# Four row tiles on GpSimd, 16-bit sine angles and a rearranged filter front in a gated-mixer kernel

## Chip, cores and metric

One core of a Trainium2 chip. The metric is the device time of one launch in microseconds (us). Engines are named as in the profile: PE is TensorE, PEld its weight loads, DVE is VectorE, ACT is ScalarE, POOL is GpSimd, SP is SyncE. "Clock" is the mean granted clock of TensorE over a run, 1.0 being full speed.

## The reference, cut to what matters

```python
def _A_ref(q, k, v, shift_k, ssm_k, ssm_D):      # S = 2048, D = 640, all bf16
    k_shift = sum(k_pad[:, t:t + S, :] * shift_k[:, 3 - t] for t in range(4))
    kv = k_shift * v
    y = irfft(rfft(kv, padded to 2S) * rfft(ssm_k, padded to 2S))[:S]
    return q * (y + kv * ssm_D)                  # ssm_D: the "skip weights"

def _B_ref(x, w1, b1, w2, b2):                   # x is q; w1: S x 1536, w2: 1536 x S
    h = layernorm(x, axis=-1)                    # 2048 rows of 640: 16 "row tiles" of 128 rows
    return transpose(gelu(einsum("bsd,sf->bdf", h, w1) + b1) @ w2 + b2)

g = sigmoid((x * gate_w).sum(-1))
return g * A + (1 - g) * B
```

## The kernel before

Transforms are matmuls against sine tables (FTB), which ScalarE makes out of integer angles (pint). Each of the five filter blocks of 128 channels is turned by eight transposes on PE and evicted into wT. A list scheduler with estimated durations fixes the order of every engine's instructions when the kernel is built; on the chip each engine then runs its list in order. These parts are touched by the change or by the argument (cuts marked):

```python
def ts(eng, o, a, s1, s2, op0, op1=None, mode=1, ...):      # tensor_scalar, one or two operations
    n = n_of(o)
    d = dve_dur(n, mode) + extra if eng == "DVE" else n / 900.0 + 0.2     # what the scheduler believes
    ...

SPIN = (7, 3, 3, 2, 2)          # "spins": matmuls on zeros ahead of the transposes of each block
...
for p in PORD:                  # angles of one sine block, int32
    pv = pint[:, p, :, 1, :]
    t_ = tt("DVE", pv, V(acol, ...), V(brow, ...), ALU.mult, mode=1)
    ts("DVE", pint[:, p, :, 0, :], pv, 1024.0, None, ALU.add, mode=2)
    pprev = ts("DVE", pa, pa, 4095, None, ALU.bitwise_and, mode=2)
    sins[p] = act(FTB[...], pa, ACT.Sin, ...)
...
def transp(h, db):              # f32 PSUM; the skip weight is folded in by a one-row matmul
    for kt in range(2):
        for p in range(4):
            dfold = h == 0 and kt == 0 and p == 0
            if dfold:
                items.append((o, ident[0:1, :], Drow[0:1, 128 * db:128 * db + 128], True, False))
            items.append((o, V(ssm, ...), ident[:, :], not dfold, True))
    m_ = mms(vt, (spin(SPIN[db]) if h == 0 else []) + items, name="wtr")
    o_ = act(V(wT, ...), ..., ACT.Copy, vt=vt, name="wT")
...
def ln_scale(a, b):             # rstd of tiles a..b-1, on GpSimd
    ts("POOL", sd[:, a:b], mv[:, a:b, 1], 1e-5, None, ALU.add, prio=0)
    tt("POOL", rstd[:, a:b], sd[:, a:b], V(cst, 1, [[0, n]]), ALU.pow, prio=0)
    ...
def ln_apply(a, b):             # normalise tiles, on VectorE
    for t in range(a, b):
        xs = X[:, t // 4, t % 4, :]
        o_ = ts("DVE", xs, xs, mv[:, t, 0:1], rstd[:, t:t + 1], ALU.subtract, ALU.mult, mode=4, ...)
...
for t in range(12):             # statistics of 12 tiles (two lines in the kernel)
    ln_tile(t // 4, t % 4)
ln_scale(0, 8); ln_apply(0, 8)
for t in range(12, 16):
    ln_tile(t // 4, t % 4)
ln_scale(8, 16); ln_apply(8, 16)
for g0 in KFP:                  # filter taps: four two-input products of 1120 elements
    tt("POOL", KF[:, g0:g0 + 5, :, :], V(cw, ...), V(m32, ...), ALU.mult, ...)
```

Of the kernel before, what the change touches and what calls it, by code (L numbers as in the profile page):

```python
# [10 lines left out]
F32 = mybir.dt.float32  # L11
I32 = mybir.dt.int32
ACT = mybir.ActivationFunctionType
ALU = mybir.AluOpType
# [4 lines left out]
class _Tracker:  # L19
# [31 lines left out]
    def regions(self, ap):  # L51
# [5 lines left out]
        apl = [tuple(p) for p in ap.ap]  # L57
        esz_ap = mybir.dt.size(ap.dtype)
        assert esz_ap == esize, "bitcast size change unsupported in tracker"
        off = ap.offset  # L60
# [8 lines left out]
        free = apl[1:]  # L69
# [213 lines left out]
    def mm(self, ps_ap, lhsT, rhs, start, stop, final_val, inc, transpose=False):  # L283
        acc_r = []
        for a in (lhsT, rhs):
            for r in self.regions(a):
                acc_r.append((r, "R"))
        acc = list(acc_r)
        ps_regs = self.regions(ps_ap)
        if start:  # L290
            for r in ps_regs:
                acc.append((r, "W"))
        need = self.deps_for("PE", acc)
        self.do_waits("PE", need)
        ins = self.nc.tensor.matmul(ps_ap, lhsT=lhsT, rhs=rhs, start=start, stop=stop, skip_group_check=True)  # L295
        src = ("eng", "PE", final_val)
        for reg, mode in acc_r:
            self.add_record(reg, "R", src)
        for r in ps_regs:
            self.add_record(r, "W", src)  # L300
        if inc:
            ins.then_inc(self.clk["PE"], 1)
            self.cnt["PE"] += 1
            assert self.cnt["PE"] == final_val, (self.cnt["PE"], final_val)
            self.hist["PE"].append(dict(self.known["PE"]))
        return ins
# [19 lines left out]
class _Sched:  # L326
# [59 lines left out]
    def run(self):  # L386
# [12 lines left out]
        pend = {e: [] for e in engs}  # L399
        free = {e: 2.4 if e == "ACT" else 0.0 for e in engs}  # L400
        port = {"DVE": 0.0, "POOL": 0.0}
        dma_free = 0.0
        avail = {}
# [108 lines left out]
def _build(nc, A_q, A_k, A_v, A_shift_k, A_ssm_k, A_ssm_D, B_x, B_w1, B_b1, B_w2, B_b2, gate_w, out):  # L512
# [10 lines left out]
    with ExitStack() as es:  # L523
# [60 lines left out]
        E_base = cur[0]  # L584
        acol = alloc("acol", [128, 2, 4], I32, at=base_of(SS))
        brow = alloc("brow", [128, 2, 128], I32, at=base_of(SS) + 64)
        dif = alloc("dif", [128, 128], I32, at=base_of(SS) + 64 + 1024)
# [7 lines left out]
        kv1 = alloc("kv1", [128, 2, 4, D], BF16, at=E_base)  # L595
        ksh = [alloc(f"ksh{i}", [128, 4, D], BF16, at=base_of(GT) + 5120 * (1 + i)) for i in range(2)]
        rows = alloc("rows", [20, 5, 512], BF16, at=base_of(GT))
        kn = [alloc(f"kn{i}", [128, 4, D], BF16, at=base_of(ring[1]) + 5120 * i) for i in range(2)]
        kp = [alloc("kp0", [128, NG, 128], BF16, at=base_of(ring[1]) + 10240), alloc("kp1", [128, NG, 128], BF16, at=base_of(GTB))]
        pint = alloc("pint", [128, 4, 2, 2, 256], I32, at=base_of(ring[1]))  # L600
        W2 = alloc("W2", [128, 32, 512], BF16, at=base_of(ring[0]))
# [77 lines left out]
        def last_stt(o, i, sc, b, vt):  # L679
# [3 lines left out]
            return SC.add("DVE", dve_dur(n_of(o), 1), emit, [sc, b], [o], vt=vt, name="fin")  # L683

        def memset(eng, ap, val, prio=None):
            return SC.add(eng, 0.2, lambda s: T.op(eng, lambda e: e.memset(ap, val), [], [ap]), [], [ap], prio=prio)  # L686

# [38 lines left out]
        def chk(ci):  # L726
            return lambda s: s[:, ci * 512:ci * 512 + 320]

        def ssm_load(h, a, b):
            dma(ssm[:, a:b, 1024 * h:1024 * h + 1024], dr(A_ssm_k, 128 * S * a + 1024 * h, [[S, 128], [128 * S, b - a], [1, 1024]]), 128 * (b - a) * 2048, chain=True, rate=(262.0 if a == 0 else 195.0) if h == 0 else 385.0)  # L730

# [6 lines left out]
        def x_load(hk):  # L738
            dma(X[:, hk, :, :], dr(A_q, 512 * hk * D, [[4 * D, 128], [1, 4 * D]]), 128 * 5120, chain=True, rate=410.0)

# [43 lines left out]
        memset("DVE", zz[:, :], 0.0, prio=-1)  # L784
        SPIN = (7, 3, 3, 2, 2)

        def spin(k):
            return [((lambda s: s[:, 0:512]), zz[:, 0:128], zz[:, :], True, True)] * k

        T_PI = float(np.float32(math.pi * (1.0 - 1e-6)))  # L790
        memset("DVE", cst[:, 0:1], T_PI)
        memset("DVE", cst[:, 1:2], -0.5)
        iota = lambda ap, pat, b, cm: SC.add("POOL", 0.2, lambda s: T.op("POOL", lambda e: e.iota(ap, pat, base=b, channel_multiplier=cm), [], [ap]), [], [ap])
        iota(dif[:, :], [[1, 128]], 0, -1)
        iota(acol[:, :, :], [[4, 2], [1, 4]], 0, 8)
        iota(brow[:, :, :], [[-512, 2], [4, 128]], 1, 0)
        iota(dif2[:, :], [[1, 32]], 128, -1)
        ts("DVE", ident[:, :], dif[:, :], 0.0, None, ALU.is_equal)
        memset("POOL", rows[0:20, 3:5, :].rearrange("g a b -> g (a b)")[:, 0:896], 0.0)
        ro, ri = V(rows, 1536, [[128, 4], [160, 4], [1, 32]], pn=20), V(rows, 0, [[1, 4], [0, 4], [4, 32]], pn=20)  # L800
        SC.add("DVE", 0.6, lambda s: T.op("DVE", lambda e: e.tensor_copy(ro, ri), [ri], [ro]), [ri], [ro], prio=0, name="taps")
        PORD = (0, 2, 1, 3)
        sins = {}
        for p in PORD:
            pv = pint[:, p, :, 1, :]
            t_ = tt("DVE", pv, V(acol, p, [[4, 2], [0, 256]]), V(brow, 0, [[0, 2], [1, 256]]), ALU.mult, mode=1)
            ts("DVE", pint[:, p, :, 0, :], pv, 1024.0, None, ALU.add, mode=2)
            pa = pint[:, p, :, :, :].rearrange("q a b c -> q (a b c)")
            if p != 0:
                t_.after.add(pprev)  # L810
            pprev = ts("DVE", pa, pa, 4095, None, ALU.bitwise_and, mode=2)
            pv3 = pa
            sins[p] = act(FTB[:, p, :, :, :, :].rearrange("q a b c d -> q (a b c d)"), pa, ACT.Sin, bias=cst[:, 0:1],
                scale=-(2.0 * math.pi / 4096.0) * (1.0 - 1e-6), name="sin")

        for hk in range(2):
# [15 lines left out]
        def consts():  # L832
# [6 lines left out]
            act(cc[:, :], lambda s: s[:, 0:28], ACT.Copy, vt=vt, name="cc")  # L839

        def transp(h, db):
            vt = _VT("cv")
            items = []
            for kt in range(2):
                for p in range(4):
                    o = (lambda s, j=4 * kt + p: s[:, 128 * j:128 * j + 128])
                    dfold = h == 0 and kt == 0 and p == 0
                    if dfold:
                        items.append((o, ident[0:1, :], Drow[0:1, 128 * db:128 * db + 128], True, False))
                    items.append((o, V(ssm, db * S + 1024 * h + 4 * kt + p, [[8, 128]]), ident[:, :], not dfold, True))  # L850
            m_ = mms(vt, (spin(SPIN[db]) if h == 0 else []) + items, name="wtr")
            m_.dur = 0.5
            o_ = act(V(wT, 2 * h * SL + 128 * db, [[SL, 2], [D, 4], [1, 128]]), (lambda s: s[:, :].rearrange("q (a b c) -> q a b c", a=2, b=4)), ACT.Copy, vt=vt, name="wT")
            if h == 0:
                o_.after.add(sins[0 if db == 0 else 2])

# [83 lines left out]

        MIXP = 330
        LNA = 8
        lnlast = []
        kfirst = []
        KFP = (0, 5, 10, 15)
        srcW = lambda h: (lambda kt, p, ci: wT[:, 2 * h + kt, p, 320 * ci:320 * ci + 320])
        for h in range(2):
            for db in range(ND):
                transp(h, db)
            if h == 0:  # L950
                consts()
# [6 lines left out]
            if h == 0:  # L958
                for t in range(8):
                    ln_tile(t // 4, t % 4)  # L960
                for t in range(8, 12):
                    ln_tile(t // 4, t % 4)
                lnlast.append(SC.ops[-1])
                ln_scale(0, LNA)
                ln_apply(0, LNA)
                lnlast.append(SC.ops[-1])
                for t in range(12, 16):
                    for o_ in ln_tile(t // 4, t % 4):
                        o_.after.update(lnlast[-1:])
                ln_scale(LNA, 16)  # L970
                ln_apply(LNA, 16)
                lnlast.append(SC.ops[-1])
                for g0 in KFP:
                    tt("POOL", KF[:, g0:g0 + 20 // len(KFP), :, :], V(cw, 7 * g0, [[7, 20 // len(KFP)], [1, 7], [0, 32]]), V(m32, 0, [[0, 20 // len(KFP)], [0, 7], [1, 32]]), ALU.mult, xr=[pv3] if g0 == 0 else []).after.update(kfirst[:1])
                    kfirst.append(SC.ops[-1])
                for hk in range(2):
                    k_turn(hk)
                mixing(C[0], SS, 0, fine=True, prio=MIXP)
            else:
                mixing(C[1], C[0], 0, conj=True, prio=MIXP)  # L980
# [338 lines left out]
```

## Time and profile before

| | before |
|---|---|
| median of 4 runs (range) | 181.96 us (181.78 to 183.0) |
| span of the profiled run, clock | 179.7 us, 1.0 |
| PE / DVE busy | 96% / 95% |
| last row tile normalised | 33.0 us |
| first eviction of the filter transform | 13.79 us |

The span in the trace is about 2 us shorter than the time of the launch. The lines of this profile are shown in the prediction.

To compare two kernels that do the same matmuls in another order I use one figure more: **matmul work done by a time t**. It is the number of 320-column matmuls begun by t, in PE's timeline, times 0.1362 us (about their pitch in unbroken runs there: 80 in 11.03 us, less the tail of the last), plus the number of key-convolution matmuls times 0.0545. Transposes and matmuls on zeros are left out. A kernel that has done 2 us less than another at the same t stands 2 us behind. It is an estimate worked out from counts.

### The profile page before, as it was taken

How to read it: one execution, taken by the hardware profiler on the slowest of the kernel's cores; microseconds unless marked ns; L12 is line 12 of the kernel's file. 1: busy time of each engine (PE TensorE's matmuls, PEld its weight loads, DVE VectorE, ACT ScalarE, POOL GpSimd, SP SyncE). 2: the span in 40 equal slices, each digit the busy share in tenths (PEclk: the TensorE clock that was granted, in tenths of full speed). 3: DMA queues.
4: the chain of work that ended last, by engine and by line, in shares of the span. 5: the costliest groups of instructions: out<-in, count | busy, mean ns of one | idle time of the engine just before them, and what ended most of it. 6: DMA issues, size and time to landing. Idle time of an engine off the chain costs nothing.

```text
span 179.7 us, 3335 instructions
## 1 busy us (share of the span) xinstructions
PE 173.1 (96%) x1381; PEld 128.7 (72%) x1381; DVE 171.2 (95%) x203; ACT 116.9 (65%) x176; POOL 43.7 (24%) x42
## 2 busy tenths in 40 slices
PE   7969998899999999999999999999999999999993
PEld 2546785587778777776777778888888887777772
DVE  7999895999999999999999899999999999999984
ACT  5899998899898999617999932131231323753760
POOL 4089404190000054000240010402525000252000
PEclk9999999999999999999999999999999999999999
DMA  6999999999999999998299969797999999599463
GB/s 151 381 411 372 388 294 194 268 420 296 212 258 286 184 271 248 229 228 218 60 243 299 197 94 365 170 225 253 166 193 217 210 200 385 218 154 240 116 233 135
DMA packets 38542, 43.51 MB, mean 242 GB/s; under 512 B 15867, under 2 KB 31360, under 8 KB 38528
## 3 DMA queue, kind: packets, MB, share of 16 engines
q1 hardware_dynamic: 33296, 32.16, 58.2%
q0 software_dynamic: 5200, 11.14, 35.6%
q8 instruction: 11, 0.18, 0.4%
q14 instruction: 3, 0.02, 0.0%
q10 hardware_dynamic: 32, 0.01, 0.0%
HBM read 25.87 MB, written 2.62 MB: 159 GB/s over the span
## 4 chain that ended last, share of the span: by engine, by line
PE 88%; ACT 10%; DVE 0%; issue 0%
PE pp L295 88%; ACT wT L670 3%; ACT C L670 2%; ACT ksh L670 2%; ACT FTB L670 2%; ACT L670 1%; ACT GT L670 0%; DVE O L682 0%; DVE zz L686 0%; ACT cw L670 0%; DVE cst L686 0%
## 5 line engine op out<-in xcount | busy, mean ns | idle before, releaser
L295 PE MATMUL pp<-X,ring 128*128 128x320 bf16 x384 | 55.6, 299 | 0.0
L626 DVE TENSOR_TENSOR C<-C 128x2560 bf16<-128x2560 bf16 (+2 forms) x37 | 54.5, 1521 | 0.0
L295 PE MATMUL pp<-GT,W 128*128 128x320 bf16 x384 | 52.6, 299 | 0.0
L295 PEld LDWEIGHTS pp<-GT,W 128*128 128x128 bf16 x384 | 43.6, 114 | 8.6
L295 PEld LDWEIGHTS pp<-X,ring 128*128 128x128 bf16 x384 | 37.1, 98 | 14.9 <-DVE X L641 0.7
L670 ACT ACTIVATE C<-pp 128x640 bf16<-128x640 f32 x64 | 40.4, 723 | 4.9 <-PE pp L295 4.9
L670 ACT ACTIVATE O<-pp,c,omg 128x640 bf16<-128x640 f32 x15 | 13.3, 884 | 34.7 <-PE pp L295 34.7
L264 POOL DMA_DIRECT2D C<-C x8 | 10.9, 1610 | 41.7 <-DVE C L626 38.3
L295 PE MATMUL pp<-wT,FTB 128*128 128x320 bf16 x112 | 17.2, 299 | 2.5 <-ACT wT L670 1.4
L670 ACT ACTIVATE cgb<-pp,gg 128x640 bf16<-128x640 f32 x16 | 12.7, 794 | 5.7 <-PE pp L295 5.3
L295 PEld LDWEIGHTS pp<-wT,FTB 128*128 128x128 bf16 x112 | 10.5, 98 | 7.7 <-ACT wT L670 1.8
L670 ACT ACTIVATE GT<-pp,cc 128x640 bf16<-128x640 f32 x12 | 9.6, 799 | 9.0 <-PE pp L295 9.0
L626 DVE TENSOR_TENSOR tm<-C,C 128x2560 bf16<-128x2560 bf16 (+1 forms) x7 | 14.3, 2057 | 0.0
L922 DVE BATCH_NORM_STATS2 stats<-X 128x6 f32<-128x320 bf16 x32 | 13.5, 461 | 0.0
L295 PE MATMUL pp<-C,FTB 128*128 128x320 bf16 x96 | 13.4, 299 | 0.0
L264 POOL DMA_DIRECT2D C<-q_hi x6 | 5.9, 977 | 27.7 <-DVE C L626 13.2
L295 PEld LDWEIGHTS pp<-C,FTB 128*128 128x128 bf16 x96 | 9.3, 98 | 3.8 <-issue 0.3
L670 ACT ACTIVATE gq<-gq 128x640 bf16<-128x640 bf16 x16 | 11.8, 741 | 0.0
L626 DVE TENSOR_TENSOR SS<-C 128x2560 bf16<-128x2560 bf16 x8 | 11.7, 1487 | 0.1
L626 DVE TENSOR_TENSOR C<-tm 128x2560 bf16<-128x2560 bf16 (+1 forms) x9 | 10.6, 1192 | 0.1
L670 ACT ACTIVATE ksh<-pp 128x1024 bf16<-128x1024 f32 (+1 forms) x12 | 9.8, 894 | 0.6 <-PE pp L295 0.6
L670 ACT ACTIVATE wT<-pp 128x1024 bf16<-128x1024 f32 x10 | 9.7, 1041 | 0.6 <-PE pp L295 0.6
(73 smaller groups left out, 193.4 us busy)
## 6 DMA issues: line engine op xcount, KB each, us to landing
ring<-in_B_w_dram SPq DMA_DIRECT2D x12, 512.0 KB, 9.6
W<-in_B_w_dram SPq DMA_DIRECT2D x12, 512.0 KB, 6.5
C<-C POOLq DMA_DIRECT2D x8, 640.0 KB, 10.6
X<-in_A_q_dram SPq DMA_DIRECT2D x4, 640.0 KB, 8.4
kn<-in_A_k_dram SPq DMA_DIRECT2D x4, 640.0 KB, 9.3
out_dram<-O SPq DMA_DIRECT2D x7, 320.0 KB, 3.5
C<-SS POOLq DMA_DIRECT2D x3, 640.0 KB, 11.4
ssm<-in_A_ssm_k_dram SPq DMA_DIRECT2D x3, 512.0 KB, 6.8
```

Source lines behind the costliest of these rows:

```text
L264: ins = engobj.dma_start(out_ap, in_ap, accum_op=ALU.add, max_dma_last_dim=2560)
L295: ins = self.nc.tensor.matmul(ps_ap, lhsT=lhsT, rhs=rhs, start=start, stop=stop, skip_group_check=True)
L626: o_ = SC.add(eng, d, lambda s: T.op(eng, lambda e: e.tensor_tensor(o, a, b, op), rd, [o]), rd, [o], prio=prio, name="tt")
L670: return T.op("ACT", lambda e: e.activation(o, src, func, **kw), rr + [src], ww)
L922: ops.append(SC.add("DVE", 0.38, (lambda o, i: lambda s: T.op("DVE", lambda e: e.bn_stats(o, i), [i], [o]))(o, i), [i], [o]))
```

## The change

The intent: take work off VectorE and ScalarE in the first 33 us, where TensorE still waits. GpSimd, 24% busy, normalises four of the sixteen row tiles while VectorE finishes all statistics; angles come from a 16-bit table; the filter is transposed into bf16 PSUM without the one-row matmul, so the skip weights are added to row 0 of wT afterwards; one filter block is evicted by VectorE; ten of the twenty matmuls on zeros go.

```diff
-        SPIN = (7, 3, 3, 2, 2)
+        SPIN = (0, 3, 0, 0, 0)                   # and four spins ahead: SP0 = 4
 for p in PORD:                                   # order of blocks 2, 0, 1, 3 instead of 0, 2, 1, 3
-            t_ = tt("DVE", pv, V(acol, ...), V(brow, ...), ALU.mult, mode=1)
-            ts("DVE", pint[:, p, :, 0, :], pv, 1024.0, None, ALU.add, mode=2)
-            pprev = ts("DVE", pa, pa, 4095, None, ALU.bitwise_and, mode=2)
+            t_ = tt("DVE", pv, V(tb, ...), V(jrow, ...), ALU.add)          # int16; jrow by GpSimd
+            pprev = ts("DVE", pa, pa, 4095, None, ALU.bitwise_and, mode=4)
 # transposes (cut)
-                    if dfold: items.append((o, ident[0:1, :], Drow[...], True, False))
+                    items.append(((lambda s, j=j: s[:, 0:512].bitcast(BF16)[...]), V(ssm, ...), ident, True, True))
+            if (h, db) in WTD:                   # WTD = ((0, 0),)
+                o_ = evac_dve(o, i, vt, prio=0)
+                if h == 0 and db in (2, 4):      # row 0 of wT, 320 columns at a time
+                    stt("DVE", o, o, 1.0, i, ALU.mult, ALU.add, prio=0)
 # row tiles
-                for t in range(12): ln_tile(...)
-                ln_scale(0, 8); ln_apply(0, 8)
-                for t in range(12, 16): ln_tile(...)
-                ln_scale(8, 16); ln_apply(8, 16)
+                for t in range(16):
+                    ln_tile(t // 4, t % 4)
+                    if t == 7: ln_scale(0, 8)
+                ln_scale(8, 16)
+                for t in PAP:                    # PAP = (0, 1, 2, 3)
+                    ts("POOL", xs, xs, mv[:, t, 0:1], rstd[:, t:t + 1], ALU.subtract, ALU.mult, prio=0)
+                for t in range(16):
+                    if t not in PAP: ln_apply(t, t + 1)
```

Cut: the table's set-up, the DMA rates and start times that the scheduler assumes, and the helpers for 16-bit PSUM.

## The prediction

> **What bounds the kernel now.** I read the page's busy shares first, then the chain of waits in order of time, then the timelines of VectorE (DVE), GpSimd (POOL), ScalarE (ACT) and TensorE (PE) for the first 45 us.
>
> ```profile
> PE 173.1 (96%) x1381; PEld 128.7 (72%) x1381; DVE 171.2 (95%) x203; ACT 116.9 (65%) x176; POOL 43.7 (24%) x42
> ```
>
> Two engines are almost full. To end earlier, both PE and DVE must do the same work earlier; freeing one does nothing alone. The chain says where it is still possible:
>
> ```profile
> 1.18 3.95 PE pp L295 x16
> ...
> 5.15 1.02 ACT wT L670
> 6.17 2.07 ACT FTB L670 x2
> 8.25 0.92 ACT wT L670
> ...
> 11.29 1.84 ACT wT L670 x2
> ...
> 13.18 16.41 PE pp L295 x142
> ...
> 33.72 1.28 ACT L670
> ...
> 37.59 3.29 ACT ksh L670 x4
> ...
> 40.93 136.12 PE pp L295 x1048
> ```
>
> From 40.93 us to 177 us the chain is matmuls without a break (1048 in 136 us). The diff leaves their number alone. So all gain must be made before 41 us: up to 13.18 us ACT sets the pace (four sine tables, five filter evictions), then PE and ACT by turns. PE work before 13.18 is mostly filler: 20 matmuls on zeros ("spins") and 40 transposes of about 70 ns. The other engines there:
>
> ```profile
> 1.51 0.69 DVE L626 TENSOR_TENSOR pint<-acol,brow 128x512 int32<-128x512 int32 x1
> 2.23 0.44 DVE L640 TENSOR_SCALAR pint<-pint 128x512 int32<-128x512 int32 x1
> 2.71 0.69 DVE L640 TENSOR_SCALAR pint<-pint 128x1024 int32<-128x1024 int32 x1
> ...
> 19.95 2.94 DVE L641 TENSOR_SCALAR X<-X,mv,rstd 128x640 bf16<-128x640 bf16 x8 [0.57 <-POOL rstd L626]
> ...
> 30.08 2.94 DVE L641 TENSOR_SCALAR X<-X,mv,rstd 128x640 bf16<-128x640 bf16 x8 [2.11 <-POOL rstd L626]
> ```
> ```profile
> 9.79 8.13 POOL L626 TENSOR_TENSOR KF<-cw,m 128x1120 bf16<-128x1120 bf16 x4 [7.00 <-DVE pint L640]
> ...
> 18.23 1.68 POOL L626 TENSOR_TENSOR rstd<-sd,cst 128x8 f32<-128x8 f32 x1
> ...
> 35.27 4.96 POOL L1031 COPY KT<-KT 128x20 bf16<-128x20 bf16 x1 [4.95 <-DMA KT<-kp]
> ```
>
> The reader should see: the sine angles cost DVE about 1.57 us per block (start to start 0.61 + 0.36 + 0.60), DVE twice waits for POOL's rstd (0.57 and 2.11 us, the number after the bracket), and the last row tile is normalised only at 33.0 us. POOL is idle most of the time.
>
> **What the Trainium skill says.** (1) "VectorE: DVE Perf Modes", The perf-mode tier table: a tensor_tensor on 16-bit SBUF data makes two results a cycle and on 32-bit data one; a 16-bit tensor_scalar makes four; anything in PSUM at most two. The trace agrees on what it has: the int32 multiply of 512 elements takes 0.69 us, about one a cycle, and the bf16 tensor_scalar on X starts every 0.37 us for 640. (2) "GPSIMD Engine Reference", 3.1: a tight one-input loop costs about 1.8 cycles per element, and 4.1 calls one-input work roughly line-rate. No instruction of this trace shows a POOL tensor_scalar of this size. (3) The same page, 1: POOL's SBUF interfaces are shared with DVE instructions that run a 2-port mode or have two SBUF inputs. The trace agrees: the POOL copy of 20 elements took 4.96 us beside DVE's tensor_tensors, a POOL memset of the same 20 elements 0.47 us. (4) "TensorE: Matmul & The Clock Gate", Part 4: transpose mode does not count as busy for the clock gate. The trace has no transpose mode yet, but has a slow start: the first seven spins take 3.14 us (0.45 each), three later ones 0.75 us start to start (0.25 each).
>
> **The change, part by part.**
>
> *16-bit angles.* Instead of an int32 multiply, add and AND per block, a small product (128) and table (256), then per block one 16-bit add of 1024 and one AND of 1024. By (1) an estimate: add 1024/1.92 GHz + 0.08 = 0.61 us, AND 1024/3.84 + 0.08 = 0.35; 0.96 x 4 + 0.75 for the base = 4.6 us against 1.57 x 4 = 6.3. DVE saves 1.7. But POOL first has to write rows of indices, and the base steps precede the first block: I count zeros and constants to 1.2 us, product, the row memset (0.47, moved from POOL), two table steps and the identity to 2.75, add and AND to 3.7. The first sine starts at 3.75, against 3.43 now.
>
> *One filter block by VectorE.* ACT loses one eviction (0.92). DVE gains one copy of 1024 from 16-bit PSUM: 0.65 us at two a cycle, 1.15 at one.
>
> *bf16 PSUM and skip weights on the row.* Five 1-row matmuls of about 0.15 us leave PE, before 13.18, where PE waits anyway: worth nothing in itself. DVE gains two one-partition operations of 320: 0.4 each, 0.8.
>
> *Fewer spins.* 20 become 10, of which three now sit inside the filter transform. Filler: worth nothing unless PE was late.
>
> *Start of the filter transform.* ACT now has four sines (1.09 start to start), four evictions (0.92) and one small one (0.2). The order puts three sines first, then the evictions, and the fourth sine after. DVE puts the filter copy between the second add and its AND, so the second and third sines wait about a microsecond: three sines end near 8.4, evictions near 12.2, the fourth sine at 13.3. The last two filter blocks land by DMA only at 9.0 us now (PE waits there 0.14 us for them) and in the same place after, so nothing before 11.2 is possible. **Transform start: 12.2 instead of 13.18; its first eviction 13.2 instead of 13.79.** Then 16 evictions at 0.61 and one small one, 9.9 us: ACT is through at 23.1, not 24.1. PE needs only 8.7 us for its 16 groups and now has no row-tile work to fill with, where it used 1.1 us for that at 21.0. So PE's own gain is about nil at 23 us.
>
> *Row tiles.* DVE starts statistics at 8.2, a little later than now (7.84), but runs all 16 tiles through: 16 x 0.86 + 0.8 + two key permutations of 0.75 + about 0.4 waiting for the keys = 24.6. POOL: filter taps (4 x 2.03) end at 16.9, scale of the first eight at 19.1, four tiles at an estimated 0.96 to 1.1 us by (2) to 23.3. PE asks for them at about 22.7: small wait. DVE does tiles 4 to 7 in 24.6 to 26.1 while POOL makes the second rstd (1.9 us, ready 26.7), then the last eight: 29.7. **Last tile 29.7 instead of 33.0.** Sum for DVE: -1.7 angles, +0.5 memset, +0.65 copy, +0.8 rows, -1.5 four tiles, -2.7 waits, +0.5 new wait = -3.4, which agrees.
>
> *What of this reaches the end.* DVE then goes to the mixing sums, but one of them needs the eighth eviction of the second filter half, which ACT delivers at 36.0 by my count (now 37.5): transposes 23.1 to 27.8, four evictions to 31.5, table load and gelu to 33.6, four more. DVE waits there about 1.4 us and keeps 1.8 of its 3.4. PE comes to the key convolution with the equivalent of 1.7 us in hand (33.7 instead of 36.55, less one group of 8 matmuls not yet done, 1.1). ACT keeps 1.5. All three meet at **1.5 to 1.8 us**, which the unbroken matmuls carry to the end: 182.0 - 1.7 = 180.3.
>
> **Rivals.** (A) *POOL is late.* The port is shared, POOL may need 1.3 us or more a tile, and the second rstd stands behind these tiles. For: the 4.96 us copy. Against: DVE runs one-input statistics meanwhile, beside which POOL's 1120-element products kept 2.03 us. Each 0.3 us a tile delays both by 1.2 us; PE has to wait: 181.5 to 182.5. (B) *Cold TensorE.* With seven fewer spins before the transform and transposes that do not count as work, the transform may begin at half clock: 0.27 instead of 0.136 us per matmul. For: the slow first spins. Against: ACT's 0.61 per group of four covers part of it, and three spins were kept. It costs up to 1.5 us: 181.8. (C) *All of DVE's gain arrives*, if ACT delivers the second half earlier, because PE mixes it better among row-tile work: 178.7. (D) *Nothing arrives*: ACT, which loses only 0.92 us of work, is the real pacer up to 41 us, and refilled static orders later cost what the front gains: 181.7.
>
> **Range and chances.** The centre is 180.3. (C) gives the low end 178.8, (A), (B) and (D) the high end 181.8; I give the stretch 8 in 10. More than 2% faster needs 3.64 us, more than DVE's whole gain: 0.07. More than 2% slower needs POOL or the cold clock to double my worst: 0.02. Within 2%: 0.91.
>
> **What would show each step.** First matmul of the transform near 12.2 (it is the group with wT and FTB on PE), its first eviction near 13.2. A 16-bit add near 0.6 us and a 16-bit AND near 0.35 us. The filter copy on DVE near 0.7. POOL's four X tiles at about 1 us each, ending by 23.5. The last X tile on DVE near 29.7 and no wait on rstd over 1 us. The last unbroken run of matmuls starting 1.5 us earlier at equal work. It is wrong if the transform starts before 11.5 or after 13, if DVE does not wait for ACT's evictions around 35 us, if matmuls of the transform take 0.27 us, or if new PE gaps open after 45 us.

## The result and the profile after

The changed kernel takes 191.28 us, median of 4 runs (190.91 to 191.68). The ratio is 1.050, 95% interval 1.0454 to 1.0546: slower. Here and below a ratio is the mean time of one kernel's fast runs over that of the other's of the same rounds, so not quite the ratio of the medians quoted. The result is correct, the profiled span 189.1 us, the clock 0.982.

First the page's busy line of the kernel after:

```profile
PE 175.3 (93%) x1366; PEld 130.5 (69%) x1366; DVE 172.9 (91%) x202; ACT 116.6 (62%) x175; POOL 52.0 (28%) x53
```

POOL is busy 8.3 us more. DVE, which was to lose work, has 1.7 us more. The chain of waits of the kernel after, in order of time (start, length, what):

```profile
10.88 2.30 DVE wT L658
...
14.56 0.90 DVE wT L658
...
19.36 1.69 POOL rstd L634
...
21.33 10.69 POOL X L649 x4
32.07 8.08 PE pp L298 x64
...
56.76 129.60 PE pp L298 x1002
```

In the chain of before there was no GpSimd step before 41 us; now one of 10.69 us stands in it: the four row tiles. Two steps of VectorE on row 0 of wT, 2.30 and 0.90 us, come before. GpSimd's timeline of the kernel after shows the same from its side (start, length):

```profile
19.36 1.68 POOL L634 TENSOR_TENSOR rstd<-sd,cst 128x8 f32<-128x8 f32 x1
...
21.32 10.70 POOL L649 TENSOR_SCALAR X<-X,mv,rstd 128x640 bf16<-128x640 bf16 x4
...
32.32 1.67 POOL L634 TENSOR_TENSOR rstd<-sd,cst 128x8 f32<-128x8 f32 x1
```

A tile takes 2.5 us and more. The second rstd, whose statistics were ready at 26.5 us, stands in GpSimd's queue behind the tiles and starts at 32.32. VectorE's timeline of the kernel after:

```profile
10.80 2.38 DVE L658 SCALAR_TENSOR_TENSOR wT<-wT,Drow 1x320 bf16<-1x320 bf16 x1
...
14.48 0.97 DVE L658 SCALAR_TENSOR_TENSOR wT<-wT,Drow 1x320 bf16<-1x320 bf16 x1
...
27.09 2.55 DVE L649 TENSOR_SCALAR X<-X,mv,rstd 128x640 bf16<-128x640 bf16 x4
34.02 2.94 DVE L649 TENSOR_SCALAR X<-X,mv,rstd 128x640 bf16<-128x640 bf16 x8 [4.38 <-POOL rstd L634]
```

VectorE waits 4.38 us for that rstd and has its last tile at 36.96 us, not at 33.0. And PE's timeline of the kernel after:

```profile
23.93 0.43 PE L298 MATMUL pp<-X,ring 128*128 128x320 bf16 x2
26.37 0.45 PE L298 MATMUL pp<-X,ring 128*128 128x320 bf16 x2 [2.01 <-POOL X L649]
29.52 0.71 PE L298 MATMUL pp<-X,ring 128*128 128x320 bf16 x2 [2.70 <-POOL X L649]
32.07 0.71 PE L298 MATMUL pp<-X,ring 128*128 128x320 bf16 x2 [1.83 <-POOL X L649]
32.57 3.48 PE L298 MATMUL pp<-ident,ssm 128*128 128x128 bf16 x32
```

PE takes two matmuls a tile and then stands still until the next: 2.01 + 2.70 + 1.83 = 6.5 us. The 32 transposes of the second filter half had long been possible; they stand behind the tiles in the fixed order, because the scheduler believed 0.91 us a tile. ScalarE, which evicts those transposes, starves with PE (7.90 us). The windows view of before and after (stretch, its length, busy time of PE, PEld, DVE, ACT, POOL with instructions, PE clock, DMA share, GB/s):

```profile
25.00:30.00 5.00, 4.84 (x44) 3.55 (x42) 2.94 (x9) 4.12 (x6) 1.85 (x2) 1.00 0.94 196
30.00:35.00 5.00, 4.64 (x33) 2.89 (x34) 4.92 (x10) 4.12 (x6) 0.25 (x2) 1.00 1.09 236
```
```profile
25.00:30.00 5.00, 0.93 (x4) 0.25 (x4) 4.61 (x10) 0.77 (x1) 5.00 (x3) 0.89 0.92 198
30.00:35.00 5.00, 3.17 (x26) 2.72 (x26) 0.97 (x3) 1.33 (x2) 4.45 (x5) 0.50 1.00 198
```

PE goes from 4.84 to 0.93 us of work in five, and its clock is then 0.50 for the next five. Matmul work done, before against after: 6.67 and 5.45 us at 20 us, 18.11 and 9.81 at 35, 32.01 and 22.72 at 50, 152.27 and 143.01 at 170. So 1.2 us of the loss are there by 20 us, 7.1 come between 20 and 35, another 1.0 by 50, and from then on the distance stays at 9.3, which is the measured difference.

### The profile page after: what moved, and what is told of

The parts are those of the page before. It is cut to its first block, busy times and chain, and to the rows that moved or that the text cites. A ratio compares the mean times of both kernels' runs of the same rounds, so it can differ in the third digit from the quotient of the medians.

```text
span 189.1 us, 3312 instructions
## 1 busy us (share of the span) xinstructions
PE 175.3 (93%) x1366; PEld 130.5 (69%) x1366; DVE 172.9 (91%) x202; ACT 116.6 (62%) x175; POOL 52.0 (28%) x53
## 4 chain that ended last, share of the span: by engine, by line
PE 79%; DVE 9%; POOL 7%; ACT 3%; issue 1%; POOLq 0%
PE pp L298 79%; POOL X L649 6%; DVE stats L954 3%; DVE wT L658 2%; ACT C L678 1%; DVE pint L634 1%; POOL rstd L634 1%; ACT GT L678 1%; DVE pint L648 1%; ACT L678 1%; DVE mv L958 1%; DVE wT L684 0%; DVE O L690 0%; DVE rows L699 0%; DVE rows L839 0%
## 5 line engine op out<-in xcount | busy, mean ns | idle before, releaser
L298 PE MATMUL pp<-X,ring 128*128 128x320 bf16 x384 | 56.2, 301 | 6.6 <-POOL X L649 6.5
L298 PE MATMUL pp<-wT,FTB 128*128 128x320 bf16 x112 | 18.7, 318 | 1.6 <-ACT wT L678 0.9
L678 ACT ACTIVATE wT<-pp 128x1024 bf16<-128x1024 bf16 x9 | 8.7, 1043 | 7.9 <-PE pp L298 7.9
L298 PEld LDWEIGHTS pp<-ident,ssm 128*128 128x128 bf16 x80 | 8.3, 163 | 3.8 <-DMA ssm<-in_A_ssm_k_dram 3.5
```

What stands on the lines that cost most here:

```text
L298: ins = self.nc.tensor.matmul(ps_ap, lhsT=lhsT, rhs=rhs, start=start, stop=stop, skip_group_check=True, is_transpose=True if ps_ap.dtype = ...
L678: return T.op("ACT", lambda e: e.activation(o, src, func, **kw), rr + [src], ww)
```

## The experiments

**Undo the row tiles, and do them alone.** Theory: GpSimd's slow tiles are the loss. Rival: the cold clock, or the front.

```diff
-  statistics of 16 tiles; POOL tiles 0..3; the rest
+  row-tile block of the kernel before                 # e1
```

> The changed kernel with only its row-tile part put back: VectorE normalises all 16 tiles, eight of them after 12 statistics, as the kernel before does; 16-bit table, bf16 PSUM, row adds, the block on VectorE and the fewer spins stay. Theory POOL (GpSimd takes 2.5 us a tile and its four tiles stand ahead of TensorE's first row-tile matmuls and of the second rstd): 180.5 to 183.5. Rival COLD (fewer spins and transpose mode leave TensorE at half clock): still 187 or more. Rival ROW (the two one-row adds, 2.38 and 0.97 us, delay the statistics): still 186 or more.

185.14 us (5 runs, 185.05 to 186.13), ratio 1.0174 (1.0157 to 1.0191). 6.1 of 9.3 us come back; 3.2 stay, which I had not expected. The profiled run, at clock 0.977, was the 186.13; the runs at 0.996 to 1.0 took 185.05 to 185.29.

The reverse, the kernel before with the new row-tile block alone:

> The kernel before with only the row-tile part of the change: four tiles on GpSimd, all statistics first, its own table, spins and f32 transposes kept. Theory POOL: 188 to 192, POOL tiles again at 2.5 us, TensorE idle 6 us or more before its first row-tile matmuls. Rivals COLD and ROW: 183 or less, as neither is in it.

190.36 us (4 runs), ratio 1.0463 (1.0432 to 1.0494). PE waits 2.87, 1.83 and 1.77 us for GpSimd's tiles. The row-tile part alone makes nearly the whole loss.

The parts do not add: 8.4 + 3.2 is 2.3 more than 9.3. Of these, 1.4 us lie at the end of e1, where the scheduler came to another order. PE's timelines of before and of e1 end with these lines, and the chain of e1 goes on behind them:

```profile
173.62 3.42 PE L295 MATMUL pp<-GT,W 128*128 128x320 bf16 x24
```
```profile
178.23 1.79 PE L298 MATMUL pp<-GT,W 128*128 128x320 bf16 x12
```
```profile
178.43 0.80 ACT cgb L678
...
179.26 0.84 DVE cgb L634
...
180.12 0.49 DVE O L634
...
180.94 0.55 DVE O L690
```

In e1 PE has only 12 matmuls left, not 24, when its last transform is done, and the last sums on ScalarE and VectorE outlast it. From the end of PE's last matmul to the end of the span it is 4.1 us (180.02 to 184.1), in the kernel before 2.7 (177.04 to 179.7). The same end stands in e5, e6, e7 and e10 (4.0 to 4.1 us); in all other runs here it is 2.7. So in the times of these five runs some 1.4 us (an estimate, from one profiled execution of each) do not belong to the part that was undone. Why the rest does not add is not shown; a late front may hide behind a late tile.

**What a GpSimd tile costs.** Four forms of the tile operation, one on each of the four tiles (wrong result; the three new forms need no rstd and run early):

```diff
+  t == 1: ts("POOL", xs, xs, mv[:, t, 0:1], None, ALU.subtract)      # one operation, operand per partition
+  t == 2: ts("POOL", xs, xs, 0.01, 20.0, ALU.subtract, ALU.mult)     # two operations, constants
+  t == 3: ts("POOL", xs, xs, 20.0, None, ALU.mult)                   # one operation, constant
```

> The changed kernel with a different instruction on each of GpSimd's four tiles, wrong result on purpose: tile 0 as it was (subtract and multiply, both by per-partition values), tile 1 subtract alone by a per-partition value, tile 2 two operations by constants, tile 3 one multiplication by a constant. If the per-partition operands cost: tile 1 well over tile 3 and tile 2 near 1 us. If the second operation costs: tiles 0 and 2 near 2.5 us, tiles 1 and 3 near 1.3 us. If it is the port shared with VectorE: all four near 2.5 us, the last one, beside an idle VectorE, shorter. If it is the element loop for bf16 in general: all four near 2.5 us.

191.21 us (one run). The view of the tile X, times in ns min/median/max:

```profile
L648 POOL TENSOR_SCALAR X<-X,mv x1: 2217/2217/2217, 11.1 to 11.1; 128x640 bf16<-128x640 bf16 x1
L649 POOL TENSOR_SCALAR X<-X x1: 2402/2402/2402, 13.4 to 13.4; 128x640 bf16<-128x640 bf16 x1
L648 POOL TENSOR_SCALAR X<-X x1: 1817/1817/1817, 15.9 to 15.9; 128x640 bf16<-128x640 bf16 x1
L649 POOL TENSOR_SCALAR X<-X,mv,rstd x1: 2784/2784/2784, 26.9 to 26.9; 128x640 bf16<-128x640 bf16 x1
```

The cheapest form takes 1.82 us; a second operation adds 0.6, an operand per partition 0.4. So the bulk goes with the 640 bf16 elements, some 2.5 ns each (a one-operation tensor_scalar of 8 f32 elements, sd, takes 0.24 us in the same run). Nor is it a fight for the port: in the kernel after the last tile ran from 29.5 to 32.0 us, while VectorE stood idle, and took 2.5 us like the others.

**Is it the cold clock?** The changed kernel with 54 filler matmuls, on data already there and into unused PSUM columns, put among the matmuls of the first three row tiles:

```diff
+  if ft == 0 and hk == 0 and p < 3:
+      for _ in range(18):
+          items.append((unused PSUM columns, ident[:, :], r[:, 0, 0:192], False, False))
```

> The changed kernel with three times 18 matmuls of 192 columns between the first four row tiles' matmuls, into unused columns, so that TensorE works while it waits for GpSimd. Theory POOL: only what the half clock added afterwards comes back, about 1.2 us (32 transposes in 3.5 us that take 2.2 us warm), so 190. Rival COLD: 186 or less.

191.76 us (4 runs), ratio 1.0547 (1.0504 to 1.059). The clock was 1.00 from 20 to 40 us, and the time did not come down: my expectation (190) missed. But the front did gain. Matmul work was 25.06 us at 50 us and 125.03 at 150, against 22.72 and 122.99 in the kernel after. It was lost after 150 us, in two waits that the kernel after does not have there (VectorE's and PE's timelines of e4):

```profile
155.61 5.82 DVE L634 TENSOR_TENSOR C<-C 128x2560 bf16<-128x2560 bf16 x4 [5.75 <-DMA C<-SS]
```
```profile
160.17 8.85 PE L298 MATMUL pp<-C,FTB 128*128 128x320 bf16 x64 [2.06 <-DVE C L634]
```

That DMA took 18.4 us from issue to landing. So the half clock and the order of PE, which the fillers changed too, together cost up to 2.3 us by 50 us; the two are not separated. Two runs at a mean clock of 1.0 took 191.06 and 192.11. As the cause of the large loss the rival is out, since 2.3 is far from 9.3; that half speed in this gap costs nothing is not shown.

**Is it only the order?** The scheduler is told the truth, 2.53 us a tile:

```diff
-  ts("POOL", xs, xs, mv[:, t, 0:1], rstd[:, t:t + 1], ALU.subtract, ALU.mult, prio=0)
+  ts("POOL", xs, xs, mv[:, t, 0:1], rstd[:, t:t + 1], ALU.subtract, ALU.mult, prio=0).dur = 2.53
```

> The changed kernel with the GpSimd tile's cost told to the kernel's own scheduler as 2.53 us instead of 0.91; work and engines the same, only the static orders change: TensorE does the second filter half before its first row tiles. If TensorE's wait in the static order is the whole loss: 182 to 183. If the late second rstd (VectorE normalises its last eight tiles at 34 us) holds too: 185 to 188.

188.67 us (4 runs, 187.6 to 190.4), ratio 1.0379 (1.0319 to 1.0439). A right estimate returns some 2.6 us, though e5 has the longer end of e1 (1.4 us). The 32 transposes now come ahead of the tiles (PE's timeline of e5), and no wait of PE for them is left in the list of waits:

```profile
24.70 2.26 PE L298 MATMUL pp<-ident,ssm 128*128 128x128 bf16 x32
```

The four tiles still end at 31.95 and the second rstd still starts at 32.26, and this part the new order does not mend.

**GpSimd's tiles, or the statistics order?** The row-tile part does two things. These two runs part them:

```diff
-  PAP = tuple(range(4))
+  PAP = ()                    # e16
+  PAP = tuple(range(2))       # e17
```

> The changed kernel with an empty list of GpSimd tiles: all sixteen statistics still come first, then VectorE normalises all sixteen tiles. Theory (GpSimd's 2.5 us a tile and the second rstd that stands behind them are the cost): statistics end at 26.5, the second rstd follows at once (done near 28.5), the last tile is done at 33 instead of 36.9, no VectorE wait on rstd over 0.5 us; TensorE waits some 3 to 4 us for the first tile (27.6). 185 to 186.5. Rival (running all statistics first is what costs, since the first tile is not there before 27 us): 188.5 or more.

> The changed kernel with two tiles on GpSimd instead of four. Theory: they end at 23.9 and 26.4, the second rstd is done near 28.4, VectorE's last tile near 32.2, earlier than in any kernel so far; TensorE waits about 3 us in all for GpSimd's and VectorE's tiles. 184.5 to 186.5, about half way back to the kernel without the row-tile part or better. Rival (any GpSimd tile in TensorE's way costs its 2.5 us and the rest is elsewhere): 188 or more.

184.95 us (4 runs, 183.9 to 185.69), ratio 1.013, and 184.6 us (4 runs, 183.54 to 185.81), ratio 1.0131 (1.008 to 1.0182). Both theories hold, both rivals fall. With two tiles instead of four 6.7 us come back. The two timelines of e17, GpSimd and VectorE:

```profile
21.32 5.00 POOL L649 TENSOR_SCALAR X<-X,mv,rstd 128x640 bf16<-128x640 bf16 x2
...
27.37 1.98 POOL L634 TENSOR_TENSOR rstd<-sd,cst 128x8 f32<-128x8 f32 x1
```
```profile
27.09 5.24 DVE L649 TENSOR_SCALAR X<-X,mv,rstd 128x640 bf16<-128x640 bf16 x14
```

Against 10.70 us of tiles and an rstd at 32.32: now it starts at 27.37, 0.9 us after its statistics, VectorE runs fourteen tiles without a gap and is done at 32.33, and no wait of PE for row tiles is left in the list of waits. So the first two tiles cost nothing against none (e16), and the third and fourth, with the rstd behind them, cost the 6.7 us.

**The 2.38 us row add.** Why does an add on one partition, 320 elements, take so long? In e1 the GpSimd and VectorE timelines give:

```profile
10.85 2.06 POOL L634 TENSOR_TENSOR KF<-cw,m 128x1120 bf16<-128x1120 bf16 x1
12.87 2.31 POOL L634 TENSOR_TENSOR KF<-cw,m 128x1120 bf16<-128x1120 bf16 x1
```
```profile
10.97 2.28 DVE L658 SCALAR_TENSOR_TENSOR wT<-wT,Drow 1x320 bf16<-1x320 bf16 x1
14.55 0.97 DVE L658 SCALAR_TENSOR_TENSOR wT<-wT,Drow 1x320 bf16<-1x320 bf16 x1
```

The first add ends at 13.25, just after a tap product of GpSimd ends (12.91); the second at 15.52, just after the next (15.18). Test: let the tap products start only after the first rstd; both adds then come ahead of them.

```diff
# on top of e1; the tap products start after the first entry of kfirst
-  ln_scale(0, LNA)
+  kfirst.append(ln_scale(0, LNA))
```

> As e1_ln_as_before, but GpSimd's four tap products start only after the first rstd, so that nothing runs on GpSimd beside VectorE's two one-row additions. If GpSimd's two-input products hold them up: 0.4 to 0.5 us each instead of 2.3 and 1.0. If one-partition additions are slow in themselves: unchanged. The total may be worse, since the products come late and VectorE normalises beside them.

191.37 us (one run): slower as a whole. But the adds now take 0.46 and 0.48 us: the rest was waiting for GpSimd's two-input products. In their new place the products hold VectorE up as well. GpSimd's and VectorE's timelines of e7:

```profile
18.87 8.88 POOL L634 TENSOR_TENSOR KF<-cw,m 128x1120 bf16<-128x1120 bf16 x4
```
```profile
19.62 3.60 DVE L649 TENSOR_SCALAR X<-X,mv,rstd 128x640 bf16<-128x640 bf16 x2
23.14 5.29 DVE L768 COPY kp<-kn 128x2560 bf16<-128x2560 bf16 x2
```

Two row tiles take 3.60 us, elsewhere 0.37 apiece; two key copies 5.29, elsewhere 0.81 apiece. So on VectorE not only two-input operations pay: these are one-input copies and tensor_scalars. (The other direction, GpSimd waiting, is the copy of 4.96 us in the kernel before; it takes 0.39 us in the kernel after.)

**Row adds on GpSimd** (e1 with the adds moved there, between the products):

```diff
-  stt("DVE", o, o, 1.0, i, ALU.mult, ALU.add, prio=0)
+  tt("POOL", o, o, i, ALU.add, prio=0)
```

> Row tiles as in the kernel before (as e1_ln_as_before), and the two one-row additions made by GpSimd between its tap products instead of by VectorE. Theory: of the 3.2 us that e1 is slower than the kernel before, most is VectorE standing 2.3 and 1.0 us in two additions of 320 elements that wait for GpSimd's product to finish; without them VectorE's last row tile ends near 33 us instead of 35.0 and the time is 182 to 183. Rival (the rest of the change, its start or its spins, costs it): still 184.5 or more.

184.7 us (4 runs, 183.27 to 185.59), ratio 1.0102 (1.0031 to 1.0173). GpSimd's adds take 0.78 us each. Some 1 us comes back by the ratios (1.0174 to 1.0102), the runs scatter, and the time is the rival's (184.5 or more): the adds are not most of e1's 3.2 us.

**The 16-bit table alone**, all else as before:

```diff
   kernel before
+  int16 table, order of blocks 2, 0, 1, 3, the zero rows set by VectorE, scheduler start times and DMA rates
```

> The 16-bit angle table alone: row tiles, f32 transposes with the folded skip weights, five evictions on ScalarE and the spins (20) as in the kernel before. VectorE should save about 1.7 us of table work, the first sine starts 0.3 us later. If the table is worth its VectorE time: 180.5 to 181.5. If ScalarE paces the front and the later first sine counts: 182 to 182.5.

181.41 us (4 runs, 180.94 to 182.15), ratio 0.9944 (0.9899 to 0.9988). Repeated in five rounds on another chip:

> e8_table_only once more, in five rounds on the same chip as the three above: 181.0 to 181.8, ratio to the kernel before 0.992 to 0.998, the bottom of the ladder. If the first time was luck, the ratio is 1.000 within 0.002.

181.4 us (6 runs, 180.72 to 182.12), ratio 0.997 (0.9943 to 0.9998). Both intervals end just under one: a gain of some 0.3 to 0.6%, the only version that beats the kernel before, and inside the 2% that counts as the same.

**A ladder through the rest.** e1 still has 3.2 us without a shown cause. Three steps from e1 towards the table alone:

```diff
-  SPIN = (0, 3, 0, 0, 0), three spins inside the transform
+  SPIN = (0, 3, 3, 4, 3), the three ahead of it        # e9, e10, e11
-  WTD = ((0, 0),)
+  WTD = ()                                             # e10, e11
-  stt("DVE", o, o, 1.0, i, ...)
+  tt("POOL", o, o, i, ALU.add, prio=0)                 # e11
```

> e1_ln_as_before (row tiles as before, the rest of the change kept; 185.1 us) with the matmuls on zeros put back: 4+3+3+4+3 = 17 of them instead of 7, none of them inside the transform. Still open is where e1's 3.2 us come from. Theory (spread over several parts): the spins hold the clock at 1.0 from 11 to 19 us in every run, which is worth the 1.0 us by which e1's one cold run (186.13) stood above its others (185.05 to 185.29), and nothing in warm runs: median 184.5 to 185.3, all mean clocks above 0.995. Rival (the missing spins are the rest of the loss): 182 to 183.

> e9_spins_back with the first filter block evicted by ScalarE again. What is left of the change against e8_table_only (181.4 us) is the 16-bit transposes and the two row adds on VectorE that wait 2.28 and 0.97 us for GpSimd. Theory: the block itself is worth little (0.69 us on VectorE for 0.9 on ScalarE): 184 to 185; the row adds keep about 2 us of wait. Rival (the VectorE block delays the second and third sine tables and with them everything): 182 to 183.

> e10_spins_act_block with the two row adds by GpSimd, as in e6_rows_on_pool. Theory: VectorE's waits of 2.28 and 0.97 us are the last large piece, and GpSimd's two adds of 0.78 us push its first rstd back by as much, so about 1.5 us come back: 182.3 to 183.3. Rival (16-bit transposes or a static order that comes out worse later cost the rest): unchanged from e10_spins_act_block within 0.5 us.

183.94 (183.85 to 185.86), 185.73 (185.4 to 186.06) and 183.6 us (182.96 to 184.0), ratios 1.0144, 1.0209 and 1.0088. By the medians the spins return 1.2 us, giving ScalarE its block back makes things *slower* by 1.8, and moving the adds to GpSimd returns 2.1; none of the three times fell where its theory or its rival had it. But e1 and e10 have the longer end shown above, and e9 and e11 have not. Less its 1.4 us, the steps are an estimated 0.2 slower, 0.4 slower and 0.7 faster: no step is worth more than 0.7 us. PE's timeline of e9 shows a wait that was in no theory:

```profile
13.66 0.38 PE L298 MATMUL pp<-ident,rows 4*128 4x4 bf16 x5 [1.92 <-DMA rows<-in_B_b_dram]
```

Five tiny transposes of the bias rows stand in the order ahead of the whole transform and wait 1.92 us for a DMA (1.2 and 0.25 in e10, 2.74 in e11). So I moved them behind the transform:

```diff
-  mms(vt, items, name="cst")
+  mms(vt, items, name="cst").after.add(wfirst[3])      # e13 = e11 + this; e14 = e13 with WTD = ((0, 0),); e15 = e10 + this
# in all three the call that makes them also moves behind the transform's
```

> e11_rows_pool_rest_undone (183.6 us) with one edit of order: the five tiny transposes of the bias rows come after the first matmul groups of the filter transform instead of ahead of all of them. Theory (the order wait is what is left): the first eviction of the transform comes at 14.0 to 14.6 instead of 16.87, and 1.5 to 2.5 us come back: 181.0 to 182.2. Rival (16-bit transposes, or the later static order, cost it): 183.3 to 184.

> e13 with the first filter block evicted by VectorE as in the change: so the whole change but for GpSimd's row tiles, with the spins kept, the row adds on GpSimd and the bias transposes late. Theory: what remains of the change is a gain, as predicted for the front (one ScalarE eviction less): 180.3 to 181.3, as good as or better than the 16-bit table alone (181.4). Rival (the VectorE block delays the second and third sine tables by about a microsecond and takes back what it gives): equal to e13 within 0.4 us.

> e10_spins_act_block (185.7 us; the row adds on VectorE, waiting 2.3 and 1.4 us for GpSimd) with the bias transposes late as in e13. Theory (the two waits are separate terms): it gains the order wait of 1.16 us plus little, 184.2 to 184.9, and stays 2 us or more above e13 because of the row adds. Rival (the order wait hides behind the row adds, so only the latter count): unchanged, 185.4 to 186.1.

183.78 (183.42 to 185.08), 184.19 (183.99 to 184.43) and 183.63 us (183.43 to 186.05), ratios 1.0097, 1.0107 and 1.0115. My theories missed in all three (e13's range was 181.0 to 182.2, e14's 180.3 to 181.3, e15's 184.2 to 184.9). In e13 the first eviction came at 14.06 us as expected, matmul work at 20 us rose from 3.40 (e11) to 6.13, nearly that of before (6.67), and the time did not move. e13 loses the distance again between 50 and 70 us (31.60 against 32.01 at 50, 50.12 against 52.17 at 70), where PE waits 0.69 us for a key DMA and 0.58 for an eviction of C in a changed order; e15 loses it between 20 and 40, where PE waits 1.43 us for VectorE's row tiles. The adds and the order wait are no separate terms: e15, with the adds on VectorE, equals e13. (Of the 2.1 us from e10 to e15, 1.4 are again e10's end.)

**Are the two terms all?** The table-alone front with the row-tile part cut to two GpSimd tiles:

```diff
   e8
-  row-tile block of the kernel before
+  row-tile block of the change, PAP = tuple(range(2))
```

> The 16-bit table alone (front as in e8_table_only, 181.4 us) with the changed row-tile part cut to two tiles on GpSimd. Theory (the front and GpSimd's last two tiles are the whole loss): matmul work done by 20 us equals that of the kernel before, the last row tile is done near 31.5 us, one microsecond earlier than in any kernel so far, and the time is 180.3 to 182.0. Rival (running all statistics first leaves TensorE without filler between 24 and 27 us, which e17 hid behind its late front): TensorE waits over 1.5 us for the row tiles there and the time is 183 or more.

182.15 us (6 runs, 181.94 to 182.6), ratio 1.001 (0.9995 to 1.0026). The time lies 0.15 us above my range, but the rival's 183 is out: PE has no listed wait for row tiles, and the kernel stands level with the one before, and 0.4 to 0.7% behind the table alone by the ratios. VectorE's timeline of e18:

```profile
25.55 4.57 DVE L649 TENSOR_SCALAR X<-X,mv,rstd 128x640 bf16<-128x640 bf16 x12
30.05 2.88 DVE L634 TENSOR_TENSOR SS<-C 128x2560 bf16<-128x2560 bf16 x2
```

Its last row tile is done at 30.1 us, 2.9 earlier than in the kernel before, and that buys nothing.

## Why the prediction was wrong

I predicted 180.3 us with 0.91 for the same and 0.02 for slower; it is 191.3. Point by point:

- **The step that failed is "four tiles at an estimated 0.96 to 1.1 us by (2) to 23.3".** A tile took 2.50 to 3.16 us, the four 10.70, and they ended at 32.0. I took the best case that "GPSIMD Engine Reference", 3.1, gives for a tight loop as the estimate of an instruction of which the trace of before had no example.
- **Rival (A) had the mechanism and not the size.** I wrote "POOL may need 1.3 us or more a tile, and the second rstd stands behind these tiles", and made it 181.5 to 182.5, 1.2 to 2.2 us above my centre (and above the 181.8 where I let the range end). Both halves came true (rstd 5.8 us after its statistics, PE waiting 6.5 us), with the tile more than twice the 1.1 us of my sum's upper end. The shared port, which I gave as the reason, was not it (the last tile took 2.5 us beside an idle VectorE). Its own rule, 1.2 us for each 0.3 us a tile, gives 6.5 us with the measured 2.67 in place of 1.05; e16 and e17 show the four tiles to be the cause of 6.7 of the 9.3 us. I also missed that a wrong estimate sits in the scheduler: PE's own filler, the 32 transposes, was put behind the tiles (e5: 2.6 us).
- **"0.4 each" for the row adds failed**: 2.38 and 0.97, waiting for GpSimd's products (0.46 in e7). I named that contention as point (3) and applied it to GpSimd alone. With it the scale of the first eight was done at 21.3 instead of 19.1, and the tiles started late.
- **Transform start 12.2, first eviction 13.2:** one matmul went ahead at 10.98, the rest ran from 12.38, and the first eviction began at 13.40. Near. The 16-bit add (0.59 to 0.67 us), the AND (0.33 to 0.44) and the filter copy (0.69) were right. But "PE's own gain is about nil" was too kind: 1.2 us of matmul work were missing at 20 us.
- **Rival (B), the cold clock,** happened twice: 0.50 at 30 to 35 us in the kernel after, whose front ran at 1.00, and 0.66 at 10 to 20 in e1's profiled run. In the gap it cost, together with the order, up to 2.3 us by 50 us (e4). In the front, e1's cold run stands 1.0 us above its others.
- **"The last tile earlier brings 1.5 to 1.8 us"** is doubtful too: in e18 the last tile came 2.9 us earlier and the time stayed. This was never reached by the change.
- **What stays open.** Of e1's 3.2 us, 1.4 are its longer end. The runs with the shorter end that keep the bf16 transposes and the row adds (e9, e11, e13, e14, e15) all take 183.6 to 184.2, about 2 us more than before, whatever becomes of spins, VectorE's block and the place of the adds; with two GpSimd tiles the new front, its fewer spins included, costs 2.45 us (e17 184.6, e18 182.15). What these runs share and the table alone lacks is the bf16 transposes, the row adds and the order that comes with them. No run parts these. I can show where e13 and e15 lost the time, not that they must.

## What to carry to other kernels

An idle engine is no free engine: before moving work to it, measure that very instruction form there, and look at what stands behind it in its queue (here a second rstd that two engines wait for). With a scheduler that works from estimates, a duration wrong by a factor of nearly three (0.91 us believed, 2.5 and more measured) costs twice, once for itself and once for the filler that is put behind it. When parts of a change are undone one by one, compare work done at a few fixed times and what follows the last matmul, since the totals do not add: here a new order at the end alone moved five runs by 1.4 us.

## What the Trainium skill lacked or had wrong

- "GPSIMD Engine Reference", 4.1, calls one-input work on GpSimd roughly line-rate. Here a bf16 tensor_scalar of 128 x 640 took 2.5 us on GpSimd and 0.37 (start to start) on VectorE, nearly seven times; even the simplest form took 1.82 us.
- The same page, 3.1, gives a best case of 1.8 cycles per element for a tight loop, by an estimate 0.96 us for 640, and no tensor_scalar. Measured by form: one operation with a constant 1.82, one with an operand per partition 2.22, two with constants 2.40, two with operands per partition 2.50 to 3.16 us. A table by form is missing.
- In "TensorE: Matmul & The Clock Gate", Part 1, nothing was found lacking: it gives an idle TensorE half the clock, and the runs agree (0.50 at 30 to 35 us, after 5 us with 0.93 us of work).
